# Small DMAs of a segment recurrence: one behind each streamed weight unit, and one load for a segment's rows and residual

## The chip, the cores and the metric

One Trainium2 chip, one core. The time is the device time of one launch in microseconds (us), as the median of several runs; before the change 2889.0 us (three runs, 2881.94 to 2899.9).

## The reference

Two branches over the same layer-normed input of 2,048 tokens and 1,024 channels, summed with the input:

```python
xn = layernorm(x)
# A: attention in 64 segments of 32 tokens, with 8 memory rows carried from segment to segment
mem = mem0
for s in range(64):
    h = concat([mem, xn[:, 32*s:32*s+32]])           # 40 rows
    q, k, v = h @ Wq, h @ Wk, h @ Wv                  # 32 heads of 128
    p = softmax(mask(q @ k.T * 128**-0.5))            # memory is seen by all, the segment is causal
    o = (p @ v) @ Wo
    mem, out[s] = o[:8], o[8:]
# B: feed-forward, 1024 -> 3584 -> 1024
b = gelu(xn @ w1 + b1) @ w2 + b2
return x + out + b
```

Each segment needs the memory rows that the segment before has put out, so the 64 segments run one after the other, and each needs all four weight matrices (32 MB in bf16).

## The kernel before

**Feed-forward part.** First the layer norm and branch B for all tokens, in four groups of 512. Its sum with the input, the residual, goes to DRAM (`R_n`), and `turn_R` rewrites it there in the layout that a segment reads: `R_d` by segment, `RL_d` by group of four segments. `keep_xT` writes the transposed layer-normed rows to DRAM, `xT_d` by segment and `xL_d` by group. The last four tiles of the residual are turned on ScalarE's queue, in segments 1 to 4 of the recurrence.

**Recurrence.** A segment's 40 rows are split: the first 24 of its own rows and the 8 memory rows make one tile of 32 (`hT`). The last 8 rows of four segments make another tile of 32, the left rows (`hL`), which is handled once in a group: its K and V in the first segment of the group (`i4 == 0`), its Q in the last one of the group before, its output projection in the last one (`i4 == 3`). The weights are cut into 64 units of 128 x 2,048 (512 KB), in the order of use: K, Q and V in two halves of eight units each, then 16 of the output projection. 43 units stay in SBUF. 21 are streamed anew in every segment into a pool of four buffers `st`, on SyncE's queue: about every third unit, three in some halves and two in others, five in the output projection. `unit_tile` is called where a unit is first used, and issues its DMA.

Within a segment `half_pass` multiplies `hT` (and `hL`) with the eight units of a half, ScalarE copies the result (`nat`, L552), and the transposes of it (`turner`, L455) are done on TensorE in the midst of the next half (`todo`, after its fourth unit). Behind Q come the scores and the softmax, spread over the second V half, then `oT`, the output projection, the copy `o_sb` (L690) and the transposition of the new memory rows into the next segment's `hT` (`put_mem`).

**Small DMAs** go on ScalarE's queue: the loads of the next segment's `hT` and `res` (64 KB each), of the group's `hL` and `resL`, the stores of `ot` (four of 24 rows by 512 bytes in each segment, sixteen more of 8 rows by 512 bytes for the left rows, after the last segment of a group), and the turns in segments 1 to 4. They are collected in a list, `later`, and all issued in one row behind the copy of the first K half of the next segment:

```python
if (w, u) == ("K", 0):
    for fn in later:
        fn()
    later.clear()
```

**Order and semaphores.** Each engine runs its instructions in the order in which they stand, and a DMA stands in its queue's order among them. All DMAs of both queues get one of eight semaphores, DMAHW0 to DMAHW7, in turn; a DMA is issued only when the DMA that had this semaphore last, eight places earlier, has landed. In addition a streamed unit waits until TensorE has read the unit that was in its buffer.

Of the kernel before, what the change touches and what calls it, by code (L numbers as in the profile page):

```python
# [2 lines left out]

# [19 lines left out]
SEG = 32  # L23
MEM = 8
NSEG = S // SEG
KT = DM // P
# [8 lines left out]
NX = 24  # L35
NL = SEG - NX
GRP = 4
NGRP = NSEG // GRP
# [35 lines left out]
def kernel(  # L74
# [16 lines left out]
    nc = tc.nc  # L91
# [3 lines left out]
    out_flat = out.rearrange("b s d -> (b s) d")  # L95
# [8 lines left out]
    w2_v = B_w2.rearrange("(fc p) d -> p fc d", p=P)  # L104

    dram = ctx.enter_context(tc.tile_pool(name="dram", bufs=1, space=bass.MemoryType.DRAM))
    xT_d = dram.tile([P, NSEG, KT * SEG], BF16, name="xT_d")
    xL_d = dram.tile([P, NGRP, KT * SEG], BF16, name="xL_d")
    R_d = dram.tile([NSEG, 4, SEG, 256], BF16, name="R_d")
    R_n = dram.tile([S, DM], BF16, name="R_n")  # L110
    RL_d = dram.tile([NGRP, 4, SEG, 256], BF16, name="RL_d")

    slabs = ctx.enter_context(tc.tile_pool(name="slabs", bufs=1))
    consts = ctx.enter_context(tc.tile_pool(name="consts", bufs=1))
# [10 lines left out]
    for j in range(4):  # L125
# [7 lines left out]
        out=mask[0:NX, 0:NX], in_=mask[0:NX, 0:NX], pattern=[[1, NX]], compare_op=ALU.is_ge,  # L133
# [12 lines left out]
        out=ml, in_=ml, pattern=[[8, GRP], [1, 8]], compare_op=ALU.is_ge, fill=MASKED, base=0, channel_multiplier=-1,  # L146
# [35 lines left out]
    NT = S // P  # L182
    with tc.tile_pool(name="ma", bufs=2) as ma, tc.tile_pool(name="mps", bufs=6, space=PSUM) as mps:
# [26 lines left out]
        for i in range(7):  # L210
            t = slab(7 + i, f"w2_{i}")[:, :].rearrange("p (c d) -> p c d", d=DM)
# [36 lines left out]
            )  # L248

        def keep_xT(tg, xnT):  # L250
            nc.sync.dma_start(out=xT_d[:, 16 * tg:16 * tg + 16, :].rearrange("p s (k t) -> p s k t", k=KT), in_=xnT)
# [6 lines left out]
            nc.sync.dma_start(  # L258
                out=xL_d[:, 4 * tg:4 * tg + 4, :], in_=xl[:, :, :, :, :].rearrange("p g k i t -> p g (k i t)")
            )  # L260

        def keep_R(ttg, rsb):
            eng = nc.scalar if ttg >= NT - 4 else nc.sync
            eng.dma_start(out=R_n[ttg * P:ttg * P + P, :], in_=rsb[:, :])

        def turn_R(eng, ttg):

            for i in range(4):
                rows = R_n[ttg * P + i * SEG:ttg * P + (i + 1) * SEG, :].rearrange("t (j c) -> t j c", j=4)
                eng.dma_start(out=R_d[4 * ttg + i].rearrange("j t c -> t j c"), in_=rows)  # L270
                eng.dma_start(
                    out=RL_d[ttg, :, NL * i:NL * i + NL, :].rearrange("j t c -> t j c"), in_=rows[NX:SEG, :, :]
                )

        def new_xnT(tg):
            return slab(18 + tg % 2, "xnT")[:, :].rearrange("p (s k t) -> p s k t", s=16, k=KT)
# [1 line left out]
        xnT = new_xnT(0)  # L278
# [14 lines left out]
        for tg in range(4):  # L293
# [41 lines left out]
            if not last:  # L335
                xnT = new_xnT(tg + 1)
# [8 lines left out]
                for t in range(4):  # L345
                    ttg = 4 * tg + t
                    xn = ln_apply(ttg + 4)
                    rsb = ma.tile([P, DM], BF16, name="rsb")
                    for nb in range(2):
                        cs = slice(nb * 512, (nb + 1) * 512)  # L350
# [14 lines left out]
                    keep_R(ttg, rsb)  # L365
                keep_xT(tg + 1, xnT)
                for t in range(4):
                    turn_R(nc.sync, 4 * tg + t)
            else:


# [4 lines left out]
                for n in range(8):  # L376
                    cs = slice((n % 2) * 512, (n % 2 + 1) * 512)
# [15 lines left out]
                for t in range(4):  # L393
                    ttg = 4 * tg + t
# [9 lines left out]
    with tc.tile_pool(name="stream", bufs=STREAM_BUFS) as stp, tc.tile_pool(name="sp", bufs=1) as sp, \  # L404
# [1 line left out]
            tc.tile_pool(name="tr", bufs=1, space=PSUM) as trp, tc.tile_pool(name="ql", bufs=1, space=PSUM) as qlp:  # L406
        nc.scalar.preload_act_table_set("natural_log_exp_and_others")

        later = []

        def unit_tile(unit):
            if IS_STREAMED[unit]:
                t = stp.tile([P, 2048], BF16, name="st")[:, :]
                nc.sync.dma_start(out=t, in_=copies[unit][:, :])
                return t
            if unit not in res_tiles:
                t = sp.tile([P, 2048], BF16, name="W_" + "_".join(map(str, unit)))[:, :]
                fetch(t, unit)
                res_tiles[unit] = t
            return res_tiles[unit]  # L420

        def load_h(s):
            hT = sp.tile([P, KT, SEG], BF16, name="hT", bufs=2)
            nc.scalar.dma_start(out=hT[:, :, :], in_=xT_d[:, s, :].rearrange("p (k t) -> p k t", k=KT))
            return hT

        def load_hL(g):
            hL = sp.tile([P, KT, SEG], BF16, name="hL")
            nc.scalar.dma_start(out=hL[:, :, :], in_=xL_d[:, g, :].rearrange("p (k t) -> p k t", k=KT))
            return hL  # L430

        def load_res(s):
            res = sp.tile([P, 256], BF16, name="res", bufs=2)
            nc.scalar.dma_start(out=res[:, :], in_=R_d[s].rearrange("j t c -> (j t) c"))
            return res

        def load_resL(g):
            res = sp.tile([P, 256], BF16, name="resL")
            nc.scalar.dma_start(out=res[:, :], in_=RL_d[g].rearrange("j t c -> (j t) c"))
            return res  # L440

        def put_mem(o_sb, hT):

# [13 lines left out]
        def by_head(t):  # L457
            return t.rearrange("p c (j t) -> p (c j) t", j=4)

        hT = load_h(0)  # L460
        hL = load_hL(0)
        res = load_res(0)
        o_sb = sp.tile([P, 256], BF16, name="o_sb")
        nc.vector.memset(o_sb[:, :], 0.0)
        for j in range(4):
# [13 lines left out]
                )  # L479

        qT = new_qT()
        nxt = {}
        for s in range(NSEG):
            g, i4 = divmod(s, GRP)
            final = s + 1 == NSEG
            if not final:
                later.append(lambda s=s: nxt.update(hT=load_h(s + 1), res=load_res(s + 1)))
            if 1 <= s <= 4:
                later.append(lambda ttg=NT - 5 + s: turn_R(nc.scalar, ttg))
            if i4 == 1 and g + 1 < NGRP:  # L490
                later.append(lambda g=g: nxt.update(hL=load_hL(g + 1)))

            if i4 == GRP - 1:
                later.append(lambda g=g: nxt.update(resL=load_resL(g)))

            left_kv = i4 == 0
            left_q = s == 0 or (i4 == GRP - 1 and g + 1 < NGRP)
# [49 lines left out]
            for w in ("K", "Q"):  # L547
                left = left_kv if w == "K" else left_q
                for u in range(2):
                    ps, psL = half_pass(w, u, left, {3: todo})  # L550
                    nat = sp.tile([P, 512], BF16, name=f"nat{u}")
                    nc.scalar.copy(out=nat[:, :], in_=ps[:, :])  # L552
                    todo = [turner(nat, "kT" if w == "K" else "qT", u)]
                    if left:
                        natL = sp.tile([P, 512], BF16, name="pr")
                        nc.vector.tensor_copy(out=natL[:, :], in_=psL[:, :])
                        todo.append(turner(natL, "kL", u) if w == "K" else turner_qL(natL, u))
                    if (w, u) == ("K", 0):
                        for fn in later:
                            fn()  # L560
                        later.clear()
            if s == 0:

                todo.append(lambda: q_left(0, qT, nxt["qL"]))
# [128 lines left out]
            nc.vector.tensor_tensor(out=ot[:, :], in0=psX[:, 0:256], in1=res[:, :], op=ALU.add)  # L693

            def store(s=s, ot=ot):
                for jq in range(4):
                    nc.scalar.dma_start(
                        out=out_flat[s * SEG:s * SEG + NX, 256 * jq:256 * jq + 256], in_=ot[32 * jq:32 * jq + NX, :]
                    )

            later.append(store)
            if left_o:
                rows_o = out_flat[g * GRP * SEG:(g + 1) * GRP * SEG, :].rearrange("(i t) d -> i t d", t=SEG)
                otL = sp.tile([P, 256], BF16, name="ot", bufs=2)
                nc.vector.tensor_tensor(out=otL[:, :], in0=psX[:, 256:512], in1=nxt["resL"][:, :], op=ALU.add)

                def store_left(otL=otL, rows_o=rows_o):
                    for jq in range(4):
                        for i in range(GRP):
                            nc.scalar.dma_start(  # L710
                                out=rows_o[i, NX:SEG, 256 * jq:256 * jq + 256],
                                in_=otL[32 * jq + NL * i:32 * jq + NL * i + NL, :],
                            )

                later.append(store_left)
# [5 lines left out]
_INS = ['A_x', 'A_mem0', 'A_Wq', 'A_Wk', 'A_Wv', 'A_Wo', 'A_seg_len', 'B_x', 'B_w1', 'B_b1', 'B_w2', 'B_b2']  # L721
_OUTS = [((1, 2048, 1024), 'bfloat16')]
# [30 lines left out]
```

## Time and profile before

| | |
|---|---|
| median of three runs | 2889.0 us |
| profiled execution | 2891.56 us, its span 2889.8 us |
| recurrence | from 440.7 us of the span to its end |
| busy: PE, DVE, ACT, POOL | 74%, 22%, 18%, 0% |
| mean granted TensorE clock | 0.898 |
| DMA moved | 791.88 MB, mean 274 GB/s |
| DMA queue of SyncE (q1), of ScalarE (q10) | 769.52 MB, 17.09 MB |
| issues of streamed units | 1344, 512 KB each |

PE is TensorE, DVE VectorE, ACT ScalarE, POOL GpSimd and SP SyncE. A name with a q behind it (ACTq, SPq) is the engine's queue, its sequencer: it waits, branches and issues DMAs, while the engine counts as idle. The DMA share is the mean busy share of the core's 16 DMA engines. In the groups of the profile, `L511 PE MATMUL acc<-st,hT` is line 511's matmul on TensorE, from a streamed unit and `hT` into `acc`. In rows of waits the numbers are the total in us, how often and the longest.

### The profile page before, as it was taken

How to read it: one execution, taken by the hardware profiler on the slowest of the kernel's cores; microseconds unless marked ns; L12 is line 12 of the kernel's file. 1: busy time of each engine (PE TensorE's matmuls, PEld its weight loads, DVE VectorE, ACT ScalarE, POOL GpSimd, SP SyncE). 2: the span in 40 equal slices, each digit the busy share in tenths (PEclk: the TensorE clock that was granted, in tenths of full speed). 3: DMA queues.
4: the chain of work that ended last, by engine and by line, in shares of the span. 5: the costliest groups of instructions: out<-in, count | busy, mean ns of one | idle time of the engine just before them, and what ended most of it. 6: DMA issues, size and time to landing. Idle time of an engine off the chain costs nothing.

```text
span 2889.8 us, 82618 instructions
## 1 busy us (share of the span) xinstructions
PE 2126.1 (74%) x37367; PEld 1090.6 (38%) x37387; DVE 627.4 (22%) x1696; ACT 509.3 (18%) x1081; POOL 10.8 (0%) x28
## 2 busy tenths in 40 slices
PE   7999986566776677767676777677676767677766
PEld 3444433333333343434343333334343333333433
DVE  7567521111111111111111111111111111111111
ACT  5235411111111111111111111111111111111111
POOL 0000000000000000000000000000000000000000
PEclk9999997889989898989888988888898888898988
DMA  9401378869898888988887889887989787888987
GB/s 321 132 28 59 119 234 278 308 229 322 282 323 281 305 302 298 317 295 310 295 309 281 318 284 324 275 313 262 321 276 330 265 319 271 307 297 300 311 298 259
DMA packets 270412, 791.88 MB, mean 274 GB/s; under 512 B 32971, under 2 KB 79083, under 8 KB 269548
## 3 DMA queue, kind: packets, MB, share of 16 engines
q1 hardware_dynamic: 230124, 769.52, 75.9%
q10 hardware_dynamic: 39936, 17.09, 2.2%
q8 instruction: 292, 4.78, 0.7%
q14 instruction: 60, 0.49, 0.1%
HBM read 772.83 MB, written 29.88 MB: 278 GB/s over the span
## 4 chain that ended last, share of the span: by engine, by line
DMA 49%; PE 42%; ACT 3%; DVE 2%; issue 2%; ACTq 1%; SPq 0%; DVEq 0%
PE acc L511 15%; DMA st<-Wc_Q 15%; DMA st<-Wc_V 13%; DMA st<-Wc_K 11%; PE sm L679 9%; PE ps L306 7%; DMA out_dram<-ot 5%; PE ps L353 5%; DMA st<-Wc_O 2%; PE tr L455 2%; PE ps L382 1%; PE acc L649 1%; ACT rc L619 1%; ACT oT L663 1%; ACT sm L616 1%
## 5 line engine op out<-in xcount | busy, mean ns | idle before, releaser
L511 PE MATMUL acc<-W,hT 128*32 128x512 bf16 x8192 | 763.8, 422 | 1.2 <-issue 1.2
L511 PE MATMUL acc<-st,hT 128*32 128x512 bf16 x4096 | 452.5, 428 | 372.1 <-DMA st<-Wc_Q 145.6
L511 PEld LDWEIGHTS <-hT 128*32 128x32 bf16 x12288 | 351.3, 102 | 835.2 <-issue 614.7
L552 ACT CAST nat<-acc 128x512 bf16<-128x512 f32 x256 | 150.1, 586 | 1242.2 <-PE acc L511 835.0
L679 PEld LDWEIGHTS <-oT 128*32 128x32 bf16 x8192 | 251.2, 109 | 132.3 <-issue 70.7
L455 PE MATMUL tr<-ident,nat 128*128 128x128 bf16 x1024 | 113.6, 241 | 158.2 <-ACT nat L552 157.8
L679 PE MATMUL sm<-W,oT 128*32 128x256 bf16 x4096 | 223.4, 315 | 3.3 <-issue 3.2
L679 PE MATMUL sm<-st,oT 128*32 128x256 bf16 x2560 | 165.5, 313 | 76.0 <-DMA st<-Wc_O 40.7
L511 PE MATMUL acc<-W,hL 128*32 128x512 bf16 x2048 | 207.1, 385 | 0.7 <-issue 0.7
L306 PE MATMUL ps<-xnT,w 128*128 128x512 bf16 x896 | 196.7, 382 | 4.3 <-ACT xnT L245 4.3
L533 DVE COPY kv<-tr 128x512 bf16<-128x512 bf16 x128 | 54.3, 424 | 651.0 <-PE tr L455 651.0
L455 PEld LDWEIGHTS <-nat 128*128 128x128 bf16 x1024 | 64.6, 105 | 280.5 <-ACT nat L552 192.0
L533 DVE COPY qT<-tr 128x512 bf16<-128x512 bf16 x128 | 54.3, 425 | 432.8 <-PE tr L455 432.8
L353 PE MATMUL ps<-w,gT 128*128 128x512 bf16 x657 | 146.2, 379 | 0.8
L306 PEld LDWEIGHTS <-w 128*128 128x128 bf16 x896 | 88.3, 99 | 111.5 <-issue 8.2
L511 PEld LDWEIGHTS <-hL 128*32 128x32 bf16 x3072 | 87.9, 98 | 64.8 <-issue 6.0
L447 DVE COPY hT<-tr 128x64 bf16<-128x64 bf16 x64 | 12.3, 191 | 435.7 <-PE tr L446 435.7
L511 PE MATMUL acc<-st,hL 128*32 128x512 bf16 x1024 | 103.4, 384 | 0.0
L353 PEld LDWEIGHTS <-gT 128*128 128x128 bf16 x672 | 65.3, 98 | 77.4 <-DVE g_u L322 0.4
L690 ACT CAST o_sb<-sm 128x256 bf16<-128x256 f32 x63 | 23.5, 372 | 391.2 <-PE sm L679 391.2
L314 ACT ACTIVATE g_xb<-ps,b1col 128x512 bf16<-128x512 f32 x112 | 77.0, 687 | 61.6 <-PE ps L306 60.5
L598 ACT ACTIVATE pr<-sm 128x448 bf16<-128x448 f32 x64 | 34.8, 544 | 298.6 <-PE sm L593 298.6
(93 smaller groups left out, 1665.4 us busy)
## 6 DMA issues: line engine op xcount, KB each, us to landing
st<-Wc_K SPq DMA_DIRECT2D x384, 512.0 KB
st<-Wc_Q SPq DMA_DIRECT2D x320, 512.0 KB
st<-Wc_V SPq DMA_DIRECT2D x320, 512.0 KB
st<-Wc_O SPq DMA_DIRECT2D x320, 512.0 KB
w<-in_B_w_dram SPq DMA_DIRECT2D x14, 1024.0 KB
W<-in_A_Wq_dram SPq DMA_DIRECT2D x11, 512.0 KB
W<-in_A_Wv_dram SPq DMA_DIRECT2D x11, 512.0 KB
W<-in_A_Wk_dram SPq DMA_DIRECT2D x10, 512.0 KB
```

What stands on the lines that cost most here:

```text
L306: nc.tensor.matmul(ps[:, :].rearrange("p (s t) -> p s t", t=SEG), lhsT=w1_sb[fb // 4][:, kt, (fb % 4) * P:(fb % 4 + 1) * P], rhs=xnT[:, :, ...
L314: nc.scalar.activation(out=xb[:, :], in_=ps[:, :], func=ACT.Identity, bias=b1col[:, fb:fb + 1], scale=1.0)
L353: nc.tensor.matmul(ps[:, :], lhsT=gts[fc // 7][:, fc % 7, t * P:(t + 1) * P], rhs=w2_sb[fc // 4][:, fc % 4, cs], start=(fc == 0), stop=(fc ...
L382: nc.tensor.matmul(pss[2 * t + nb][:, :], lhsT=gts[fc // 7][:, fc % 7, t * P:(t + 1) * P], rhs=w2_sb[fc // 4][:, fc % 4, nb * 512:nb * 512 ...
L455: nc.tensor.transpose(dst[:, c, :], nat[:, c * P:(c + 1) * P], ident[:, :])
L511: nc.tensor.matmul(acc[32 * j:32 * j + 32, :], lhsT=lhs[:, i, :], rhs=t[:, 512 * j:512 * j + 512], start=(i == 0), stop=(i == KT - 1), til ...
L533: nc.vector.tensor_copy(out=dst[:, :, 0:32], in_=by_head(tr[:, :, :]))
L552: nc.scalar.copy(out=nat[:, :], in_=ps[:, :])
L598: nc.scalar.activation(out=pr, in_=psS[:, 0:448], func=ACT.Exp, scale=INV_SQRT_DH)
L616: nc.scalar.activation(out=dA, in_=dA, func=ACT.Ln)
L619: nc.scalar.activation(out=rc, in_=dA, func=ACT.Exp, scale=-1.0)
L679: nc.tensor.matmul(psX[32 * jq:32 * jq + 32, o:o + 256], lhsT=lhs[:, c, :], rhs=t[:, 1024 * k + 256 * jq:1024 * k + 256 * jq + 256], start ...
```

## The change

The list `later` is replaced by a queue, `small`. `unit_tile` takes one entry out of it each time it has issued a streamed unit, so up to 21 in a segment. The loads are put at its head, the stores and turns at its end. `hT` and `res` of a segment lie side by side in DRAM (`hr_d`) and are one load of 128 x 512, as are `hL` of a group and `resL` of the group before (`hrL_d`).

```diff
-    xT_d = dram.tile([P, NSEG, KT * SEG], BF16, name="xT_d")
-    xL_d = dram.tile([P, NGRP, KT * SEG], BF16, name="xL_d")
-    R_d = dram.tile([NSEG, 4, SEG, 256], BF16, name="R_d")
+    hr_d = dram.tile([NSEG, P, 512], BF16, name="hr_d")
+    hrL_d = dram.tile([NGRP + 1, P, 512], BF16, name="hrL_d")
     R_n = dram.tile([S, DM], BF16, name="R_n")
-    RL_d = dram.tile([NGRP, 4, SEG, 256], BF16, name="RL_d")
...
         def keep_xT(tg, xnT):
-            nc.sync.dma_start(out=xT_d[:, 16 * tg:16 * tg + 16, :].rearrange("p s (k t) -> p s k t", k=KT), in_=xnT)
+            nc.sync.dma_start(
+                out=hr_d[16 * tg:16 * tg + 16, :, 0:256].rearrange("s p c -> p s c"),
+                in_=xnT.rearrange("p s k t -> p s (k t)"),
+            )
...
-        def turn_R(eng, ttg):
+        def turn_R(ttg, small=None):
             for i in range(4):
                 rows = R_n[ttg * P + i * SEG:ttg * P + (i + 1) * SEG, :].rearrange("t (j c) -> t j c", j=4)
-                eng.dma_start(out=R_d[4 * ttg + i].rearrange("j t c -> t j c"), in_=rows)
-                eng.dma_start(
-                    out=RL_d[ttg, :, NL * i:NL * i + NL, :].rearrange("j t c -> t j c"), in_=rows[NX:SEG, :, :]
-                )
+                dst = hr_d[4 * ttg + i, :, 256:512].rearrange("(j t) c -> t j c", j=4)
+                dstL = hrL_d[ttg + 1, :, 256:512].rearrange("(j t) c -> t j c", j=4)[NL * i:NL * i + NL, :, :]
+                for o, r in ((dst, rows), (dstL, rows[NX:SEG, :, :])):
+                    if small is None:
+                        nc.sync.dma_start(out=o, in_=r)
+                    else:
+                        small.append(lambda o=o, r=r: nc.scalar.dma_start(out=o, in_=r))
...
-        later = []
+        small = deque()
         def unit_tile(unit):
             if IS_STREAMED[unit]:
                 t = stp.tile([P, 2048], BF16, name="st")[:, :]
                 nc.sync.dma_start(out=t, in_=copies[unit][:, :])
+                if small:
+                    small.popleft()()
                 return t
...
+        def load_hr(s):
+            hr = sp.tile([P, 512], BF16, name="hr", bufs=2)
+            nc.scalar.dma_start(out=hr[:, :], in_=hr_d[s])
+            nxt["hT"] = hr[:, 0:256].rearrange("p (k t) -> p k t", k=KT)
+            nxt["res"] = hr[:, 256:512]
...
             if not final:
-                later.append(lambda s=s: nxt.update(hT=load_h(s + 1), res=load_res(s + 1)))
+                small.appendleft(lambda s=s: load_hr(s + 1))
             if 1 <= s <= 4:
-                later.append(lambda ttg=NT - 5 + s: turn_R(nc.scalar, ttg))
-            if i4 == 1 and g + 1 < NGRP:
-                later.append(lambda g=g: nxt.update(hL=load_hL(g + 1)))
-            if i4 == GRP - 1:
-                later.append(lambda g=g: nxt.update(resL=load_resL(g)))
+                turn_R(NT - 5 + s, small)
+            if i4 == 1:
+                small.appendleft(lambda g=g: load_hrL(g + 1))
...
-                    if (w, u) == ("K", 0):
-                        for fn in later:
-                            fn()
-                        later.clear()
...
-            def store(s=s, ot=ot):
-                for jq in range(4):
-                    nc.scalar.dma_start(
-                        out=out_flat[s * SEG:s * SEG + NX, 256 * jq:256 * jq + 256], in_=ot[32 * jq:32 * jq + NX, :]
-                    )
-            later.append(store)
+            for jq in range(4):
+                o = out_flat[s * SEG:s * SEG + NX, 256 * jq:256 * jq + 256]
+                small.append(lambda o=o, r=ot[32 * jq:32 * jq + NX, :]: nc.scalar.dma_start(out=o, in_=r))
...
-        for fn in later:
-            fn()
+        while small:
+            small.popleft()()
```

The sixteen stores of the left rows (L710) are appended to `small` in the same way.

ScalarE at the start of segment 32, the first of a group, whose small DMAs are the most (the numbers behind `nat` are buffer numbers). Before:

```order
L690 CAST o_sb<-sm 128x256
L552 CAST nat_25700<-acc 128x512
L697 DMA out_dram<-ot 24x256 x4
L710 DMA out_dram<-ot 8x256 x16
L424 DMA hT<-xT_d 128x256
L434 DMA res<-R_d 128x256
L552 CAST nat_25814<-acc 128x512
L552 CAST nat_25869<-acc 128x512
L552 CAST nat_25916<-acc 128x512
L598 ACTIVATE pr<-sm 128x448
```

After, at the same place:

```order
L686 CAST o_sb<-sm 128x256
L433 DMA hr<-hr_d 128x512
L693 DMA out_dram<-ot 24x256 x2
L552 CAST nat_25620<-acc 128x512
L693 DMA out_dram<-ot 24x256 x2
L703 DMA out_dram<-ot 8x256
L552 CAST nat_25713<-acc 128x512
L703 DMA out_dram<-ot 8x256 x2
L552 CAST nat_25770<-acc 128x512
L703 DMA out_dram<-ot 8x256 x3
L552 CAST nat_25820<-acc 128x512
L703 DMA out_dram<-ot 8x256 x3
```

The four copies of K and Q, which stood behind the row of 22 DMAs but for the first, now have the load and two stores ahead of them and two or three DMAs between each two; of the other seven stores two stand ahead of the softmax's sums and five behind the copies into `oL`.

SyncE's queue at the same place, the units of Q and the first ones of V, with the semaphores that each waits for (a unit waits for its own semaphore's last DMA, and for the last DMA into its buffer where that isn't told already; PE is TensorE's reading of the buffer). Before:

```order
L414 DMA st_25827<-Wc_Q_2_0_103 128x2048 [waits DMAHW3_49,PE_49]
L414 DMA st_25855<-Wc_Q_5_0_104 128x2048 [waits DMAHW4_49,PE_49]
L414 DMA st_25872<-Wc_Q_0_1_105 128x2048 [waits DMAHW5_49,DMAHW1_49,PE_49]
L414 DMA st_25886<-Wc_Q_3_1_106 128x2048 [waits DMAHW6_49,DMAHW5_49,PE_49]
L414 DMA st_25906<-Wc_Q_6_1_107 128x2048 [waits DMAHW7_49,DMAHW2_49,PE_49]
L414 DMA st_25928<-Wc_V_1_0_108 128x2048 [waits DMAHW2_49,PE_49]
```

After:

```order
L421 DMA st_25726<-Wc_Q_2_0_101 128x2048 [waits DMAHW2_49,PE_49]
L421 DMA st_25755<-Wc_Q_5_0_102 128x2048 [waits DMAHW4_49,DMAHW3_49,PE_49]
L421 DMA st_25773<-Wc_Q_0_1_103 128x2048 [waits DMAHW6_49,DMAHW5_49,PE_49]
L421 DMA st_25788<-Wc_Q_3_1_104 128x2048 [waits DMAHW7_49,DMAHW0_49,PE_49]
L421 DMA st_25809<-Wc_Q_6_1_105 128x2048 [waits DMAHW2_49,DMAHW1_49,PE_49]
L421 DMA st_25832<-Wc_V_1_0_106 128x2048 [waits DMAHW4_49,DMAHW3_49,PE_49]
```

SyncE's own order stays. Before, three to four small DMAs stand between `Q_0_1`, `Q_3_1` and `Q_6_1` in the turn of the semaphores, and seven between `Q_6_1` and `V_1_0`. After, the numbers step on by one to three from unit to unit, with none to two small DMAs between.

More of the change, by code (lines that the diff above doesn't have):

```diff
@@ L1 @@
 import math
+from collections import deque
 from contextlib import ExitStack
@@ L258, in keep_xT @@
             nc.sync.dma_start(
-                out=xL_d[:, 4 * tg:4 * tg + 4, :], in_=xl[:, :, :, :, :].rearrange("p g k i t -> p g (k i t)")
+                out=hrL_d[4 * tg:4 * tg + 4, :, 0:256].rearrange("g p c -> p g c"),
+                in_=xl[:, :, :, :, :].rearrange("p g k i t -> p g (k i t)"),
             )
@@ L367 @@
                 for t in range(4):
-                    turn_R(nc.sync, 4 * tg + t)
+                    turn_R(4 * tg + t)
             else:
@@ L420, in unit_tile, with load_hrL @@
             return res_tiles[unit]
[L422 to L440, printed above, removed]
+        def load_hr(s):
[3 more added lines that the diff above has]
+            nxt["res"] = hr[:, 256:512]
+        def load_hrL(g):
+            hr = sp.tile([P, 512], BF16, name="hrL")
+            cs = slice(256 if g == NGRP else 0, 256 if g == 0 else 512)
+            nc.scalar.dma_start(out=hr[:, cs], in_=hrL_d[g, :, cs])
+            nxt["hL"] = hr[:, 0:256].rearrange("p (k t) -> p k t", k=KT)
+            nxt["resL"] = hr[:, 256:512]
         def put_mem(o_sb, hT):
@@ L458, in by_head @@
             return t.rearrange("p c (j t) -> p (c j) t", j=4)
-        hT = load_h(0)
-        hL = load_hL(0)
-        res = load_res(0)
+        nxt = {}
+        load_hr(0)
+        load_hrL(0)
+        hT, res, hL = nxt["hT"], nxt["res"], nxt["hL"]
         o_sb = sp.tile([P, 256], BF16, name="o_sb")
@@ L481 @@
         qT = new_qT()
-        nxt = {}
         for s in range(NSEG):
@@ L692 @@
             ot = sp.tile([P, 256], BF16, name="ot", bufs=2)
-            nc.vector.tensor_tensor(out=ot[:, :], in0=psX[:, 0:256], in1=res[:, :], op=ALU.add)
-            def store(s=s, ot=ot):
-                for jq in range(4):
-                    nc.scalar.dma_start(
-                        out=out_flat[s * SEG:s * SEG + NX, 256 * jq:256 * jq + 256], in_=ot[32 * jq:32 * jq + NX, :]
-                    )
-            later.append(store)
+            nc.vector.tensor_tensor(out=ot[:, :], in0=psX[:, 0:256], in1=res, op=ALU.add)
+            for jq in range(4):
+                o = out_flat[s * SEG:s * SEG + NX, 256 * jq:256 * jq + 256]
+                small.append(lambda o=o, r=ot[32 * jq:32 * jq + NX, :]: nc.scalar.dma_start(out=o, in_=r))
             if left_o:
@@ L704 @@
                 otL = sp.tile([P, 256], BF16, name="ot", bufs=2)
[L705 to L715, printed above, removed]
+                nc.vector.tensor_tensor(out=otL[:, :], in0=psX[:, 256:512], in1=nxt["resL"], op=ALU.add)
+                for jq in range(4):
+                    for i in range(GRP):
+                        o = rows_o[i, NX:SEG, 256 * jq:256 * jq + 256]
+                        r = otL[32 * jq + NL * i:32 * jq + NL * i + NL, :]
+                        small.append(lambda o=o, r=r: nc.scalar.dma_start(out=o, in_=r))
             if not final:
                 hT, res, qT = nxt["hT"], nxt["res"], nxt["qT"]
-        for fn in later:
-            fn()
+        while small:
+            small.popleft()()
 _INS = ['A_x', 'A_mem0', 'A_Wq', 'A_Wk', 'A_Wv', 'A_Wo', 'A_seg_len', 'B_x', 'B_w1', 'B_b1', 'B_w2', 'B_b2']
```

## The prediction

> **What bounds the kernel now.** I read the page first, then stretches of the recurrence, then the waits, then one bad stretch by itself. The page's slices and its chain of work that ended last:
>
> ```profile
> PE   7999986566776677767676777677676767677766
> DMA  9401378869898888988887889887989787888987
> PE acc L511 15%; DMA st<-Wc_Q 15%; DMA st<-Wc_V 13%; DMA st<-Wc_K 11%; PE sm L679 9%; PE ps L306 7%; DMA out_dram<-ot 5%; PE ps L353 5%; DMA st<-Wc_O 2%; PE tr L455 2%; PE ps L382 1%; PE acc L649 1%; ACT rc L619 1%; ACT oT L663 1%; ACT sm L616 1%
> ```
>
> After the first six slices (the feed-forward part) the DMA engines are eight or nine tenths busy and TensorE six or seven. The chain runs through the streamed weights (15, 13, 11 and 2%), and 5% of it lies in `out_dram<-ot`, the stores, a few kilobytes each, which nobody should have to wait for.
>
> Next, stretches from one `o_sb` copy to the next, which is one segment each: s = 32 to 35, then the four in which the last rows are also turned (s = 1 to 4). Columns: length, busy time of TensorE, weight load, VectorE, ScalarE, GpSimd, granted clock, DMA share, GB/s.
>
> ```profile
> 1666.00:1709.00 43.00, 30.49 (x606) 16.46 (x606) 8.60 (x22) 5.47 (x14) 0.00 (x0) 0.84 0.73 253
> 1709.00:1744.17 35.17, 24.17 (x470) 11.90 (x470) 4.73 (x15) 5.47 (x13) 0.00 (x0) 0.90 0.91 328
> 1744.17:1779.09 34.92, 24.95 (x470) 12.26 (x470) 4.74 (x15) 5.48 (x13) 0.00 (x0) 0.85 0.91 318
> 1779.09:1815.24 36.15, 28.72 (x670) 16.70 (x670) 6.12 (x17) 5.48 (x13) 0.00 (x0) 0.95 0.94 324
> ```
>
> ```profile
> 482.45:521.98 39.53, 26.27 (x470) 12.80 (x470) 4.65 (x15) 5.47 (x13) 0.00 (x0) 0.75 0.81 275
> 521.98:561.19 39.21, 23.49 (x470) 11.57 (x470) 4.74 (x15) 5.58 (x14) 0.00 (x0) 0.87 0.86 299
> 561.19:607.25 46.06, 30.75 (x670) 17.40 (x670) 6.12 (x17) 5.47 (x13) 0.00 (x0) 0.85 0.78 262
> 607.25:655.41 48.16, 29.49 (x606) 15.24 (x606) 8.60 (x22) 5.48 (x13) 0.00 (x0) 0.82 0.67 226
> ```
>
> I call the four places in a group of four A (i4 = 0), B, C and D. In B, C and D the DMA engines are 0.91 to 0.94 busy: little is idle there. In A they are 0.73 busy and TensorE has 43.00 - 30.49 = 12.5 us without a matmul, so neither is the limit. Thirteen of each kind (s = 8 to 59), A, B, C and D in turn:
>
> ```profile
> sum 552.48, PE 388.41 PEld 205.24 DVE 111.77 ACT 71.21 POOL 0.00; mean PE 29.88 PEld 15.79 DVE 8.60 ACT 5.48 POOL 0.00
> sum 467.70, PE 314.76 PEld 154.36 DVE 61.48 ACT 71.19 POOL 0.00; mean PE 24.21 PEld 11.87 DVE 4.73 ACT 5.48 POOL 0.00
> sum 453.64, PE 311.78 PEld 155.90 DVE 61.66 ACT 71.20 POOL 0.00; mean PE 23.98 PEld 11.99 DVE 4.74 ACT 5.48 POOL 0.00
> sum 494.92, PE 384.93 PEld 220.96 DVE 79.65 ACT 71.29 POOL 0.00; mean PE 29.61 PEld 17.00 DVE 6.13 ACT 5.48 POOL 0.00
> ```
>
> Divided by 13: 42.5, 36.0, 34.9 and 38.1 us, 151.4 us for a group. What happens in A, seen on the timeline of ScalarE and its queue, then on TensorE's (start, length, idle time before and what ended it), then on the chain:
>
> ```profile
> 1671.24 2.38 ACTq L697 DMA_DIRECT2D out_dram<-ot  x4
> 1673.71 9.88 ACTq L710 DMA_DIRECT2D out_dram<-ot  x16
> 1683.65 0.37 ACTq L424 DMA_DIRECT2D hT<-xT_d  x1
> 1684.48 0.36 ACTq L434 DMA_DIRECT2D res<-R_d  x1
> 1684.93 0.59 ACT L552 CAST nat<-acc 128x512 bf16<-128x512 f32 x1 [13.18 <-DMA out_dram<-ot]
> ```
>
> ```profile
> 1685.57 0.61 PE L455 MATMUL tr<-ident,nat 128*128 128x128 bf16 x4 [8.63 <-ACT nat L552]
> ```
>
> ```profile
> 1671.62 5.46 DMA out_dram<-ot
> 1677.13 3.35 DMA st<-Wc_Q
> 1680.49 3.96 DMA out_dram<-ot
> ```
>
> The twenty stores of the segment before (4 at L697, 16 at L710) and two loads stand in one row on ScalarE's queue, behind the copy of the first K half. All DMAs of both queues take eight semaphores in turn, so each waits until the DMA eight places earlier has landed. The three rows of the chain have issue to landing: 5.46, 3.35 and 3.96 us, one after the other. So the row needs 13.2 us; the copy of the second K half stands behind it, and TensorE waits 8.63 us for that at its transposes. SyncE's later Q units wait for semaphores of the stores, so the stream stops as well. The totals:
>
> ```profile
> ACT nat L552 <- DMA out_dram<-ot: 237.4, 33, 14.3
> PE tr L455 <- ACT nat L552: 157.8, 30, 13.1
> PE acc L511 <- DMA st<-Wc_Q: 145.6, 123, 4.0
> PE acc L511 <- DMA st<-Wc_K: 127.4, 184, 2.3
> PE acc L511 <- DMA st<-Wc_V: 76.6, 119, 2.1
> SPq L414 <- DMA out_dram<-ot: 191.3, 83, 5.9
> ```
>
> Q and V stream five units per segment each, yet TensorE waits 145.6 us for Q's and 76.6 for V's. The burst stands just ahead of Q: the difference, 69.0 us, I put down to it.
>
> **The change, part by part.** *Stores and loads one at a time.* The same 512 stores (256 and 256) are issued, but in A only 2 or 3 stand between two copies, and five at one place, where 22 DMAs stood in a row. Their issue stays 0.28 to 0.38 us each:
>
> ```profile
> L697 ACTq DMA_DIRECT2D out_dram<-ot x256: 308/375/1535, 487.3 to 2881.8; - x128
> L710 ACTq DMA_DIRECT2D out_dram<-ot x256: 282/306/1162, 613.5 to 2887.5; - x128
> ```
>
> Three between two copies are about 1 us on a queue whose engine is 5.5 us busy in 43; TensorE's half pass hides that, and it costs nothing. Five stand behind the `oL` copies, 1.6 us beside the output projection, hidden as well. If the cover failed, at 0.3 us each for 20, A would get 6 us back. At the end the last twenty stores still go in a row (until 2887.5), as before.
>
> **Term 1, segments A.** The stall of 8.63 us goes, and with it the 16-engine share of 0.73. What is late next is the stream: 0.73 x 43.00 = 31.4 us of engine work has to pass. At a share of 0.90, a little under B's and C's 0.91 since TensorE is busier, that takes 34.9 us. Against the mean of 42.5 it is 7.6 us, in the 15 segments A that have the sixteen stores (s = 4 to 60): 114 us. Bounds: at 0.94, the best row above, 33.4 us and 137 us; at 0.86, as in the row of s = 2, 36.5 us and 90 us.
>
> Beside it a row of the same view for the stretch just after the stall:
>
> ```profile
> 1686.30:1689.70 3.40, 3.01 (x28) 1.23 (x31) 0.76 (x2) 0.49 (x1) 0.00 (x0) 0.50 0.09 23
> ```
>
> TensorE runs at a granted clock of 0.50 for 3.4 us after the stall, half speed, so some 1.7 us are lost behind it. It is no term of its own, as the engine work decides; if TensorE decided instead, 15 x 1.7 = 26 us more would go, and I use that for the low end only. The Trainium skill, "TensorE: Matmul & The Clock Gate", Part 1, says that an idle window of about 3.4 us halves the clock until about as long a busy one has passed; the trace agrees (8.63 us idle, then 0.50). By that rule A gains up to the 26 us more, without it nothing beside term 1.
>
> **Term 2, the Q units.** 69.0 us by the two rows of waits. B, C and D have a burst of six to eight DMAs, and their DMA share has little room, so this is all I take there: about 1.4 us in each of 48. Bounds: nothing, and 80 us if all three reach D's 0.94 (engine work 32.0 + 31.8 + 34.0 = 97.8 us, / 0.94 = 104.0, against 36.0 + 34.9 + 38.1 = 109.0: 5.0 a group).
>
> **Term 3, s = 1 to 4.** They are 3.5, 4.3, 8.0 and 5.7 us over their kinds' means, 21.5 us, with eight DRAM transfers more in the burst. These still have to run; two thirds of the excess go: 14 us (bounds 7 and 21).
>
> *The joined load.* 64 loads of `hT` and `res` become 64 of both, and the segment's left rows likewise. The issue of about 0.4 us goes from an engine that is not the limit, and the bytes stay: nothing. The load now leads the segment on ScalarE's queue and waits for `ot` of the segment before, which VectorE adds right behind the `o_sb` copy; behind it stand two stores and the first copy of K, which comes 5.2 us after `o_sb` (1671.24 against 1666.00). Nothing waits longer.
>
> *Feed-forward part.* `keep_xT` now writes rows of 512 bytes (2,048 of them) where each partition had 8 KB in one piece.
>
> ```profile
> L251 SPq DMA_DIRECT2D xT_d<-xnT x4: 383/384/2498, 38.6 to 322.2; - x4
> L270 SPq DMA_DIRECT2D R_d<-R_n x48: 515/522/1201, 123.7 to 343.6; - x48
> ```
>
> ```profile
> 0.00:440.70 440.70, 401.29 (x1913) 185.44 (x1933) 240.38 (x593) 158.70 (x250) 10.78 (x28) 0.98 0.46 152
> ```
>
> The nearest row with pieces of 512 bytes is the turn at L270, 128 of them: 0.52 us to issue. Sixteen times that is 8 us, four times over 33 us at most, at least nothing. I take nothing: the DMA engines are 0.46 busy there, TensorE 401 of 441 us, and no matmul of that part reads what is written. If that cover failed, up to 33 us come back.
>
> **Sum.** 114 + 69 + 14 = 197 us. The profiled execution took 2891.6 us (span 2889.8), 2.6 above the median of 2889.0; 2891.6 - 197 = 2694.6, and beside the median 2692. I say 2690.
>
> **Rivals.** *The DMA engines are the limit already.* For it: 0.91 to 0.94 in B, C and D. Then term 2 is nothing, A stops at 36.5 us (90 us) and half of term 3 remains (7 us): 2891.6 - 97 = 2795. Against it: the share of 0.94 in D shows that there is some room.
>
> *Semaphores held longer: slower.* A small transfer in the midst of a running stream takes about as long to land as a unit of the stream (5.46 against 3.35 us above). In A, 21 units and 21 small ones now alternate, so the eight semaphores pass through 42 DMAs: 42/8 x 5.5 us = 29 us, under the 34.9 of the forecast, so they don't decide. They do from 34.9 x 8/42 = 6.6 us a DMA, and with 9 us A takes 47.3 us, 4.8 over now: 15 x 4.8 = 72 us slower, 2964. B to D have 25 to 27 DMAs and 27/8 x 9 = 30 us, no change. For it:
>
> ```profile
> 1690.74 5.16 DMA st<-Wc_V
> 1707.67 6.33 DMA st<-Wc_K
> ```
>
> 6.33 us occurs in the undisturbed stream. Against it: the small transfers of a segment A add some 240 KB (48 + 64 + 128) to the 11 MB of its 21 units, and 6.33 is the longest of the rows shown but one of five. The Trainium skill, "DMA: Bandwidth & Descriptors", Queues, rings and completion order, says that a completion is signalled only after all earlier writes of that engine, across its queues. By that rule a store's landing follows the streams ahead of it, which speaks for this rival and against spreading the stores; the row of 5.46 us for 12 KB agrees.
>
> *It isn't spread.* ScalarE issues whatever stands next, with no regard to when SyncE issues its unit; the stores could bunch as before, before each copy. Then the stall is only cut in pieces, and no more than term 3 goes: 2878 to 2892. Against it: at most five stand together, and eight semaphores hold them without a second round.
>
> **How the numbers follow.** Forecast 0.70, the engines as limit 0.16, semaphores slower 0.08, not spread 0.06. A measurement of this kernel can tell about 1% (29 us) from no change; the three runs lie 0.6% apart. Faster by over 1%: 0.70 + 0.16 = 0.86; within 1%: 0.06; slower: 0.08. Low end: a share of 0.94 in all kinds. Engine work of a group is 31.4 + 97.8 = 129.2 us, / 0.94 = 137.4, 14.0 below 151.4, times 16 = 224, with 21 of term 3 and 26 of the clock 271: 2620. High end: the first rival with 10 us of the feed-forward bound: 2805. What is left out is 0.14 and a little of the forecast.
>
> **What would show it.** In the profile after: the wait of `nat` for `out_dram<-ot` near nothing (237.4 now), transposes for `nat` near nothing (157.8), the wait for Q's units near V's, A's stretch at 34 to 36 us with a DMA share near 0.90 and no stretch at clock 0.50, B and C at 33 to 35 us. It would be wrong if A's stretch stays over 40 us, with SyncE's queue waiting for `out_dram<-ot`, or if the DMA share of B to D rises without their getting shorter (more engine work for the same bytes).

## The result and the profile after

| | before | after |
|---|---|---|
| median of 4 runs each, same chip | 2891.05 us (2881.94 to 2899.9) | 2717.81 us (2702.39 to 2728.76) |
| ratio, 95% interval | | 0.9397 (0.9341 to 0.9453) |
| profiled execution's span | 2889.8 us | 2719.4 us |
| mean granted clock | 0.898 | 0.936 |

173 us went, 6.0%. Forecast were 2690 us, so the measured time is 28 us above that and within the range of 2620 to 2805. From the page of the changed kernel, the slices of the DMA engines and the chain by line:

```profile
DMA  9512177889899998999999999898989898998897
DMA st<-Wc_V 18%; PE acc L511 14%; DMA st<-Wc_Q 12%; DMA st<-Wc_K 12%; PE sm L675 8%; PE ps L313 7%; PE ps L360 5%; DMA st<-Wc_O 5%; PE ps L389 1%; PE tr L458 1%; PE acc L645 1%; ACT rc L615 1%; ACT oT L659 1%; ACT sm L612 1%; DMA out_dram<-ot 1%
```

The stores have gone from 5% of the chain to 1%. The stretches of s = 32 to 35 and of s = 1 to 4, columns as in the prediction:

```profile
1581.36:1616.07 34.71, 28.04 (x606) 14.75 (x606) 8.59 (x22) 5.48 (x14) 0.00 (x0) 1.00 0.91 318
1616.07:1650.55 34.48, 22.24 (x470) 11.30 (x470) 4.75 (x15) 5.47 (x13) 0.00 (x0) 0.95 0.94 322
1650.55:1684.36 33.81, 22.43 (x470) 11.17 (x470) 4.75 (x15) 5.48 (x14) 0.00 (x0) 0.95 0.95 338
1684.36:1722.63 38.27, 29.25 (x670) 17.57 (x670) 6.13 (x17) 5.48 (x13) 0.00 (x0) 0.96 0.88 305
...
481.52:517.75 36.23, 25.58 (x470) 12.80 (x470) 4.66 (x15) 5.48 (x13) 0.00 (x0) 0.80 0.89 317
517.75:554.98 37.23, 23.52 (x470) 11.68 (x470) 4.75 (x15) 5.57 (x13) 0.00 (x0) 0.91 0.86 309
554.98:596.13 41.15, 32.81 (x670) 18.10 (x670) 6.13 (x17) 5.48 (x13) 0.00 (x0) 0.83 0.83 297
596.13:629.73 33.60, 27.33 (x606) 14.78 (x606) 8.59 (x22) 5.48 (x13) 0.00 (x0) 0.99 0.91 322
```

The first A shown (s = 32) has nearly the DMA share of its neighbours now, 0.91 for 0.73, and a clock of 1.00 for 0.84. Thirteen of each kind, A to D in turn:

```profile
sum 452.01, PE 367.65 PEld 197.26 DVE 111.80 ACT 71.29 POOL 0.00; mean PE 28.28 PEld 15.17 DVE 8.60 ACT 5.48 POOL 0.00
sum 449.81, PE 302.25 PEld 150.87 DVE 61.75 ACT 71.19 POOL 0.00; mean PE 23.25 PEld 11.61 DVE 4.75 ACT 5.48 POOL 0.00
sum 445.24, PE 304.95 PEld 152.78 DVE 61.76 ACT 71.30 POOL 0.00; mean PE 23.46 PEld 11.75 DVE 4.75 ACT 5.48 POOL 0.00
sum 485.33, PE 380.63 PEld 222.16 DVE 79.72 ACT 71.19 POOL 0.00; mean PE 29.28 PEld 17.09 DVE 6.13 ACT 5.48 POOL 0.00
```

Means of 34.8, 34.6, 34.2 and 37.3 us, against 42.5, 36.0, 34.9 and 38.1. ScalarE in segment 32, whose burst took 13.2 us before (timeline; q is its queue):

```profile
1582.74 0.36 ACTq L433 DMA_DIRECT2D hr<-hr_d  x1
1583.14 0.99 ACTq L693 DMA_DIRECT2D out_dram<-ot  x2
1585.89 0.59 ACT L552 CAST nat<-acc 128x512 bf16<-128x512 f32 x1 [4.15 <-DMA hr<-hr_d]
1585.91 0.89 ACTq L693 DMA_DIRECT2D out_dram<-ot  x2
1589.03 0.28 ACTq L703 DMA_DIRECT2D out_dram<-ot  x1
1591.14 0.59 ACT L552 CAST nat<-acc 128x512 bf16<-128x512 f32 x1 [4.67 <-DMA out_dram<-ot]
1591.17 1.10 ACTq L703 DMA_DIRECT2D out_dram<-ot  x2
1594.94 0.59 ACT L552 CAST nat<-acc 128x512 bf16<-128x512 f32 x1 [3.21 <-PE acc L511]
```

The copies follow each other by 5.3 and 3.8 us, where the second had come 13.8 us after the first. The waits of the whole run, then SyncE's queue, then the group of the transposes:

```profile
ACT nat L552 <- DMA out_dram<-ot: 199.3, 51, 6.0
PE acc L511 <- DMA st<-Wc_K: 144.3, 196, 2.6
PE acc L511 <- DMA st<-Wc_Q: 118.6, 142, 3.2
PE acc L511 <- DMA st<-Wc_V: 99.9, 144, 2.5
```

```profile
SPq L421 <- DMA hr<-hr_d: 89.8, 51, 3.7
SPq L421 <- DMA out_dram<-ot: 41.2, 37, 4.8
```

```profile
L458 PE MATMUL tr<-ident,nat 128*128 128x128 bf16 x1024 | 106.0, 229 | 0.0
```

The transposes wait for nothing any more (the last column, their idle time before, is 0.0; it was 157.8 us for `nat` alone). ScalarE's copies are still put down to landings of stores for 199.3 us, but that does not reach TensorE's transposes: they come only after the fourth unit of the next half. SyncE's wait for stores fell from 191.3 to 41.2 us, but one wait grew: it stands 89.8 us, 51 times, for the load of `hr`, where it stood 51.3 us, 18 times, for `hT` and `res`.

### The profile page after: what moved, and what is told of

It reads as the page before. It is cut to its first block, busy times and chain, and to the rows that moved or that the text cites. A ratio compares the mean times of both kernels' runs of the same rounds, so it can differ in the third digit from the quotient of the medians.

```text
span 2719.4 us, 82557 instructions
## 1 busy us (share of the span) xinstructions
PE 2082.5 (77%) x37387; PEld 1079.0 (40%) x37387; DVE 628.0 (23%) x1696; ACT 509.1 (19%) x1081; POOL 10.8 (0%) x28
## 4 chain that ended last, share of the span: by engine, by line
DMA 50%; PE 42%; ACT 4%; DVE 2%; issue 2%; ACTq 0%; SPq 0%; DVEq 0%
DMA st<-Wc_V 18%; PE acc L511 14%; DMA st<-Wc_Q 12%; DMA st<-Wc_K 12%; PE sm L675 8%; PE ps L313 7%; PE ps L360 5%; DMA st<-Wc_O 5%; PE ps L389 1%; PE tr L458 1%; PE acc L645 1%; ACT rc L615 1%; ACT oT L659 1%; ACT sm L612 1%; DMA out_dram<-ot 1%
## 5 line engine op out<-in xcount | busy, mean ns | idle before, releaser
L511 PE MATMUL acc<-W,hr 128*32 128x512 bf16 x8192 | 731.7, 405 | 1.6 <-issue 1.6
L511 PE MATMUL acc<-st,hr 128*32 128x512 bf16 x4096 | 434.4, 410 | 387.9 <-DMA st<-Wc_K 144.3
L511 PEld LDWEIGHTS <-hr 128*32 128x32 bf16 x12288 | 345.0, 99 | 832.8 <-issue 596.6
L511 PE MATMUL acc<-W,hrL 128*32 128x512 bf16 x2048 | 205.1, 384 | 0.0
L450 DVE COPY hr<-tr 128x64 bf16<-128x64 bf16 x64 | 12.3, 192 | 449.5 <-PE tr L449 442.8
L511 PEld LDWEIGHTS <-hrL 128*32 128x32 bf16 x3072 | 86.5, 98 | 63.0 <-issue 3.6
L458 PE MATMUL tr<-ident,nat 128*128 128x128 bf16 x1024 | 106.0, 229 | 0.0
L511 PE MATMUL acc<-st,hrL 128*32 128x512 bf16 x1024 | 102.9, 385 | 0.0
L594 ACT ACTIVATE pr<-sm 128x448 bf16<-128x448 f32 x64 | 34.8, 544 | 335.8 <-PE sm L589 335.8
```

Source lines behind the costliest of these rows:

```text
L458: nc.tensor.transpose(dst[:, c, :], nat[:, c * P:(c + 1) * P], ident[:, :])
L511: nc.tensor.matmul(acc[32 * j:32 * j + 32, :], lhsT=lhs[:, i, :], rhs=t[:, 512 * j:512 * j + 512], start=(i == 0), stop=(i == KT - 1), til ...
L594: nc.scalar.activation(out=pr, in_=psS[:, 0:448], func=ACT.Exp, scale=INV_SQRT_DH)
```

## The experiments

All times are medians on the chip, beside runs of the kernel before on the same chip. Means of A to D are of the same thirteen segments each; profiles of different series come from different chips, on which the kernel before took 2891 to 2906 us. The theory: DMAs in one row land one after the other, eight semaphores apart, and both ScalarE's copies and the stream stand behind that; cutting the row is the gain. The rivals: the joined load is part of it, or the stores as such burden the stream. The first four kernels ran together (before: 2905.9 us).

**The joined loads alone**, the burst kept: `small` is emptied behind the first K half, as `later` was, with the loads behind the stores again.

```diff
-                if small:
-                    small.popleft()()
...
+                    if (w, u) == ("K", 0):
+                        while small:
+                            small.popleft()()
```

> The joined loads alone; all small DMAs still go in one row behind the first K half. Theory (the gain comes from cutting the row of DMAs that land one after the other): the row in segment A has 21 DMAs in place of 22, so A stays at 41.5 to 42.5 us and the whole at 2865 to 2890. Rival (fewer, larger loads are what made B, C and D shorter): B to D shorten by 0.9 us each as in the changed kernel, the whole 2835 to 2850.

2872.7 us, ratio 0.9875 (0.9837 to 0.9913). That is as expected, 33 us by the medians under the kernel before on its own chip. A's mean is 42.05 us, and the stall is there:

```profile
PE tr L456 <- ACT nat L550: 138.4, 18, 13.4
```

B and C stayed at 36.0 and 35.0 us and D went from 38.1 to 37.4, so the rival, 0.9 us in each, fell. That the gain comes from the shorter row is likely, but not shown.

**The spread alone**, with the two separate loads and the DRAM layout of before (`hT` and `res` each one entry of `small`).

> The small DMAs one behind each streamed unit, but with the two separate loads of before. Theory: as the changed kernel, A 34 to 36 us, the whole 2710 to 2735. Rival (the joined load carries the gain of B, C and D, 44 us): 2755 to 2770.

2695.4 us, ratio 0.9271 (0.9233 to 0.9309), better than expected. A to D are 34.7, 34.3, 33.2 and 37.1 us, so B to D take 104.7 in all, where the changed kernel has 106.2. The spread alone brings all of the gain, and more than the changed kernel on the first chip; I tested that below.

**Only the sixteen left stores spread**, one taken out by `unit_tile` behind each streamed unit, the other DMAs kept in the row.

```diff
-                later.append(store_left)
...
+                        small.append(lambda o=o, r=r: nc.scalar.dma_start(out=o, in_=r))
```

> Only the sixteen stores of the left rows are taken out of the row and go one behind each streamed unit; everything else stays in the row. Theory: A loses its stall of 8.6 us and falls to 35 to 36.5 us, B to D and segments 1 to 3 stay as before: 2775 to 2795. Rival (any row of six or more DMAs there stalls ScalarE for long, the sixteen only lengthen it a little): A 38 to 40 us, 2820 to 2850.

2812.3 us, ratio 0.9663 (0.9626 to 0.9701), 94 us under before. A's thirteen stretches, and the wait for the copies:

```profile
sum 469.82, PE 370.81 PEld 198.94 DVE 112.00 ACT 71.19 POOL 0.00; mean PE 28.52 PEld 15.30 DVE 8.62 ACT 5.48 POOL 0.00
```

```profile
PE tr L459 <- ACT nat L556: 61.0, 27, 8.4
```

36.1 us in A, as the theory had it. B and C stayed (36.1 and 35.1), but D rose from 38.1 to 39.1, and the whole is above the expected 2775 to 2795. The row of six DMAs left still holds the transposes now and then. Still, more than half of the change's gain lies in these sixteen stores.

**The stores on another queue**: the kernel before, with `nc.gpsimd` for `nc.scalar` in its two stores. GpSimd's DMAs take semaphores of their own.

> The kernel before with its stores issued from GpSimd's queue in the same bursts; these DMAs take other semaphores than the stream's. Two parts of the stall are taken away together: ScalarE no longer stands behind the stores, and SyncE's units no longer wait for semaphores of the stores. Theory: that is all the burst costs, so A 34 to 36 us, B to D 1 us under before, segments 1 to 4 still long, the whole 2715 to 2750. Rival (the stores themselves cost the stream, as many small writes among large reads on the same engines): A stays over 38 us, 2810 or more.

2690.4 us, ratio 0.9254 (0.9225 to 0.9283), less than the theory expected. In its profile no streamed unit waits for a store any more (191.3 us before). A falls to 34.3 us with the same bytes in the same bursts, once neither ScalarE nor the stream's semaphores stand behind them: the rival is out. By its ratio it beats the changed kernel without any spreading; both are put on one chip at the end.

The next four ran together (before: 2902.9 us). **The changed kernel and the spread alone, side by side:**

> The changed kernel once more, beside the spread without joined loads, since the two were timed on different chips (ratios 0.940 and 0.927). If the joined load does nothing, both come out within 0.6%; if it costs the spread kernel something, the changed one is 1% or more (25 us) behind.

> The spread with the two separate loads again, on the same chip as the changed kernel. Theory (a joined load changes only which unit waits for which small DMA): within 0.6% of it, either way. Rival (a load of 128 KB lands later than two of 64 KB, and a Q unit of the stream waits for it): 1% or more ahead of it.

2723.9 us, 0.9378 (0.9334 to 0.9422), and 2703.0 us, 0.9315 (0.9269 to 0.9361). The spread alone is 21 us (0.8%) ahead, between the two expectations and with intervals that just overlap; the direction is that of the first two chips. B to D agree: 106.6 us a group in the changed kernel and 105.0 in the spread alone, 1.6 us or sixteen times that, 25 us. SyncE's waits in the changed kernel, then in the spread alone:

```profile
SPq L421 <- DMA hr<-hr_d: 115.5, 58, 4.0
SPq L421 <- DMA out_dram<-ot: 36.9, 35, 3.0
```

```profile
SPq L418 <- DMA out_dram<-ot: 95.8, 59, 4.5
SPq L418 <- DMA hT<-xT_d: 68.3, 30, 3.9
SPq L418 <- DMA res<-R_d: 30.9, 16, 3.5
```

Their sums, 152 and 195 us, are the wrong way round, so the total of these waits is not the price.

**The changed kernel with its stores on GpSimd's queue** (`nc.gpsimd` in both `small.append` of stores):

> The changed kernel with its stores issued from GpSimd's queue: they take other semaphores than the stream and the loads, so a unit no longer waits for a store and ScalarE no longer issues any. Theory (what is left of waits on small DMAs in the changed kernel, SyncE for hr and out_dram 131 us and ScalarE for out_dram 199 us, is hidden behind DMA engines that are 0.9 busy): 0 to 15 us under the changed kernel. Rival (these waits still cost): 40 us or more under it.

2691.8 us, 0.9279 (0.9236 to 0.9321): 32 us under the changed kernel on this chip, between the two expectations, nearer to the rival's. Of SyncE's waits in streamed units, none for `out_dram` is left, and 0.6 us for `hr`, once. B, C and D:

```profile
sum 445.90, PE 308.81 PEld 156.80 DVE 61.65 ACT 71.19 POOL 26.10; mean PE 23.75 PEld 12.06 DVE 4.74 ACT 5.48 POOL 2.01
sum 434.63, PE 300.16 PEld 150.07 DVE 61.66 ACT 71.30 POOL 25.98; mean PE 23.09 PEld 11.54 DVE 4.74 ACT 5.48 POOL 2.00
sum 483.14, PE 386.06 PEld 224.97 DVE 79.65 ACT 71.20 POOL 26.01; mean PE 29.70 PEld 17.30 DVE 6.13 ACT 5.48 POOL 2.00
```

34.3, 33.4 and 37.2 us, 104.9 in all; before 109.0, changed kernel on this chip 106.6. The waits that remained were not all hidden.

**The burst kept, the copies behind it on VectorE:**

```diff
-                    nc.scalar.copy(out=nat[:, :], in_=ps[:, :])
+                    nat_copy = nc.vector.tensor_copy if (w, u) in (("K", 1), ("Q", 0)) else nc.scalar.copy
+                    nat_copy(out=nat[:, :], in_=ps[:, :])
```

> The kernel before, its burst kept, but the two copies that stood behind the burst (second K half, first Q half) are made by VectorE. It tells the two parts of the stall apart: TensorE no longer waits for ScalarE, while SyncE's units still wait for semaphores of the stores. Theory (most of the 8.6 us in A is ScalarE's place in the queue): A falls to 36 to 38 us, B to D stay, the whole 90 to 110 us under before. Rival (the units that wait for the stores' semaphores stop TensorE for as long): A stays at 41 us or more, less than 30 us under before.

2838.4 us, 0.9786 (0.9738 to 0.9833), 65 us under before: less than the theory's 90, more than the rival's 30. A's thirteen stretches, and the waits of TensorE and of SyncE:

```profile
sum 499.95, PE 390.26 PEld 205.86 DVE 128.54 ACT 55.97 POOL 0.00; mean PE 30.02 PEld 15.84 DVE 9.89 ACT 4.31 POOL 0.00
```

```profile
PE acc L511 <- DMA st<-Wc_Q: 211.0, 170, 4.2
```

```profile
SPq L414 <- DMA out_dram<-ot: 231.2, 105, 6.0
```

38.5 us in A: 4.0 of the 7.7 us go with ScalarE's place in the queue. The other half stays, and TensorE's wait for Q's units rises from 145.6 to 211.0 us while SyncE waits for stores (231.2 us for 191.3). The chain of segment 32 in this run shows where:

```profile
1639.24 5.69 DMA st<-Wc_Q
1644.94 3.54 DMA out_dram<-ot
1648.54 4.04 DMA st<-Wc_Q
```

A Q unit is issued only when a store has landed, and no copy of ScalarE lies between: the stream's semaphores are a stall of their own, which had lain behind the first one. B to D rose by 1.0 us a group (110.0 for 109.0), part of why the whole gained less than the theory's 90 us.

The last four ran together (before: 2895.5 us). **The changed kernel again, three buffers for its load, and these with the stores on GpSimd's queue.** For room, `o_sb` shares a buffer with the reciprocals `rc` in both kernels with three buffers:

```diff
-            hr = sp.tile([P, 512], BF16, name="hr", bufs=2)
+            hr = sp.tile([P, 512], BF16, name="hr", bufs=3)
```

> The changed kernel as the yardstick of the next three on the same chip: a ratio of 0.938 to 0.940 to the kernel before.

> The changed kernel with three buffers for the joined load instead of two (o_sb shares the buffer of the reciprocals for room). In the changed kernel the load stands 1.4 us behind o_sb, since its buffer still holds the residual of the segment before until VectorE has added it; with three it is issued at once. Theory (the joined load costs the spread kernel its 0.8% by that wait, passed on to the Q unit eight places behind): the load at 0.0 to 0.4 us after o_sb, the wait of SyncE for hr under 80 us (115 in the changed kernel), the whole 12 to 25 us under the changed kernel. Rival (a load of 128 KB lands 0.7 us later than one of 64 KB, and that is what costs): within 6 us of it.

> Both: stores from GpSimd's queue and three buffers. No unit waits for a small DMA any more in either, so by the theory the third buffer brings nothing on top: 28 to 40 us under the changed kernel. Rival (the two add up): 45 us or more under it.

Changed kernel 2731.5 us, 0.9422 (0.9394 to 0.9450), a little above what was expected. Three buffers 2716.3 us, 0.9372 (0.9343 to 0.9401), 15 us under it, with intervals that just overlap. The load is issued earlier, with two buffers (segment of the side-by-side run) and with three:

```profile
1618.87 0.37 ACT L686 CAST o_sb<-sm 128x256 bf16<-128x256 f32 x1 [4.82 <-PE sm L675]
1620.28 0.36 ACTq L433 DMA_DIRECT2D hr<-hr_d  x1
```

```profile
1604.44 0.37 ACT L686 CAST o_sb<-sm 128x256 bf16<-128x256 f32 x1 [4.65 <-PE sm L675]
1604.86 0.45 ACTq L433 DMA_DIRECT2D hr<-hr_d  x1
```

But the wait for it did not fall to under 80 us. In the changed kernel on this chip it is 99.2 us, 56 times, and that for stores 35.0; with three buffers it only comes less often:

```profile
SPq L421 <- DMA hr<-hr_d: 102.6, 39, 4.8
SPq L421 <- DMA out_dram<-ot: 61.7, 33, 4.8
```

So the time came out as the theory had it and the wait did not: the 15 us are no proof of the theory. Why the joined load costs the spread kernel some 20 us stays open. It does lie on the chain: the load of 1620.28 above takes 7.37 us there (`1620.28 7.37 DMA hr<-hr_d`), and the chain by line in the profile of that run has 3% in `hr`. With the stores on GpSimd's queue the third buffer brought nothing: 2692.9 us, 0.9289 (0.9257 to 0.9321), as the theory had it.

**The kernel before with its stores on GpSimd's queue, on the same chip:**

> The kernel before with nothing changed but the stores' queue (GpSimd's), beside the changed kernel on one chip. If the spreading matters only for DMAs that share the stream's semaphores, this equals the changed kernel with its stores on GpSimd's queue: 25 to 40 us under the changed kernel. If the loads' burst still costs: 15 us or less under it.

2693.2 us, 0.9298 (0.9273 to 0.9322): 38 us under the changed kernel, as expected, and level with the kernel that has the spread, the joined loads and the stores on GpSimd's queue (2692.9). A's thirteen stretches, and the longest wait that SyncE has left on small DMAs:

```profile
sum 444.99, PE 364.47 PEld 197.88 DVE 111.91 ACT 71.12 POOL 129.85; mean PE 28.04 PEld 15.22 DVE 8.61 ACT 5.47 POOL 9.99
```

```profile
SPq L414 <- DMA hT<-xT_d: 47.1, 29, 6.0
```

34.2 us in A, with GpSimd 10.0 us busy on its twenty stores, beside everything else.

## Why the prediction was right, and where its terms were off

**Term 1, segments A: right in size.** 42.5 to 34.8 us, 7.7 for the 7.6 forecast, 15 x 7.7 = 116 us for 114. I had named both ScalarE's queue and the stream's semaphores, but only the first as what stops TensorE in the stall of 8.63 us; the copies on VectorE show that it is 4.0 of the 7.7 us. The size came out since I had not summed stalls but the engine work that has to pass: 0.91 x 34.71 = 31.6 us in s = 32 after, 31.4 before. That it came out to 0.1 us is partly luck. The share of 0.90 was a choice between 0.86 and 0.94, and the mean of the thirteen is 0.89.

**Term 2, the Q units: too large, as far as the runs show because of the joined load.** B, C and D shortened by 1.4, 0.7 and 0.7 us, 2.8 a group or 44 us, for the 69 that I took from Q's wait less V's. The step that failed is *The joined load*, which I put at nothing ("Nothing waits longer"). With the two separate loads B to D lose 4.3 us a group in the first run of that kernel and 3.9 in the second (69 and 63 us), and beside the second the joined load costs 21 us of the whole. One thing that waits longer is seen: the load stands 1.4 us behind `o_sb`, until the residual of the segment before has been added, and SyncE's units then wait for it. But three buffers took that away without shortening SyncE's wait, so how the joined load costs its time stays open. With the stores on GpSimd's queue, joined load and all, B to D lose 4.1 us a group, 65 us.

That the term nearly holds without the joined load does not make its working right. In the rows of waits Q's went down by 27 us, not by 69, while K's and V's rose by 17 and 23; a difference of two rows was no price.

**Term 3, s = 1 to 4: right in size, the closeness luck.** 173.0 to 148.2 us for the four, 24.8; their kinds' own gains make up 7.7 + 1.4 + 0.7 + 0.7 = 10.5, so 14.3 are left for the 14 forecast. In the profiles of the two later series the same kernel takes 140.4 and 144.5 us for the four, and the same sum gives 23 and 18 us.

**Sum.** 116 + 44 + 14 = 174 us, against 170.4 between the two spans. *Feed-forward part:* the first streamed matmul starts at 440.7 us before and 441.0 after, so the rows of 512 bytes that it writes cost nothing, as forecast.

**The signs.** The transposes' wait went to 0.0, no A stretch as a whole stands at a low clock (0.91 to 1.00 in all thirteen), and A to C lie where I put them. Q's wait came near V's (118.6 and 99.9 us), in part since V's rose. The wait of `nat` for stores did not go to near nothing (199.3 us); I took a row of waits for a price, while four units of slack lie between the copy and who needs it.

**The rivals.** *The DMA engines are the limit already* would have been 2795. A third of term 2 did stay away, but the kernels with separate loads or with GpSimd's queue got most of it, so the engines had room for it. *Semaphores held longer* did not come: units of the stream in segment 32 after take this long to land (rows of the chain), below the 6.6 us from which it would decide. Over the recurrence the units on the chain take 5.5 us in the mean, before and after, and one in ten of them takes more than 6.6:

```profile
1585.61 6.36 DMA st<-Wc_Q
...
1594.45 4.71 DMA st<-Wc_V
...
1610.34 4.58 DMA st<-Wc_O
```

*It isn't spread* fell with the timeline above.

## What to carry to other kernels

Here a burst of small DMAs cost what stood behind it: the instructions behind it on the issuing engine, and the DMAs of both queues that took its semaphores next. Before spreading such a burst, look whether its DMAs can go through a queue with semaphores of its own; here that alone gave 0.930 of the time, where spreading with the joined load gave 0.942 on the same chip. For a stage at a shared limit, count what must pass through it rather than the stalls: the work gave A's new length, with some luck, to 0.1 us, while the difference of two rows of waits missed B to D's gain by a factor of 1.6. And try the parts of a change one by one: joining the loads, which seemed free, took back some 20 us of what the spread gave.

## What I had not expected of the hardware

Beside the running stream a small transfer does not land much sooner than a large one. On the chain of before the stores of 4 and 12 KB take 3.9 us in the mean, where the 512 KB units take 5.5; in the side-by-side run of the changed kernel the loads of 128 KB on the chain take 6.3 and the units 5.5. GpSimd's queue, with 20 stores in 34 us and 10.0 us of its own time, held up no copy, matmul or streamed unit that the rows of waits show. And a joined load, one DMA for two, was worth 33 us in a burst and cost 21 us in the spread.
